# Converting each half of w1 and w2 in one set of instructions, with a later request for one v, and the look at the weights' range taken out of ScalarE's gaps

## The chip, the core and the metric

The kernel runs on one core of a Trainium2 chip. The core has a TensorE (PE, matrix products; its weight loads are listed as PEld), a VectorE (DVE), a ScalarE (ACT), a GpSimd (POOL) and a SyncE (SP), which here issues every DMA. The engines run side by side, each through its own list of instructions in order, and wait for each other by semaphores. The metric is the device time of one execution in microseconds; of the kernel before there are three runs, 464.53, 464.53 and 465.14 us, with a median of 464.53 us.

## What is computed

The reference has two parts. The first is a gated linear attention over 4 batches of 8 heads, 768 steps, head size 48:

```
f = 1 / (1 + exp(-f_logit))
for t in range(S):
    state = f[:, :, t, :, None] * state + einsum('bhd,bhe->bhde', k[:, :, t], v[:, :, t])
    y[:, :, t] = einsum('bhd,bhde->bhe', q[:, :, t], state)
```

Its result is laid out as x with 3072 rows and 384 columns, and goes through a feed-forward part whose only product of activations is elementwise:

```
a = x @ w1            # 384 x 1024
b = x @ w2            # 384 x 1024
h = a * b @ w3        # 1024 x 1024
out = h @ w_out       # 1024 x 384
```

The weights arrive as 64-bit floats. The kernel reads them as pairs of 32-bit words and makes 32-bit floats of them itself.

## The kernel before

**The work.** The sequence is cut into 24 chunks u = 0 to 23 of 128 steps. For each chunk DVE runs two scans over the gates (lines 523 and 545) and scales q and k by them (539, 553), PE multiplies the pairs within the chunk (566 or 576), ACT copies the products out (697 or 700), POOL masks them (706), PE multiplies them with v (604 or 650, 610, 669) and brings the state forward (622 or 683), DVE keeps the state (756, 759, 815), and ACT takes the result out (842). Four chunks make a block of 512 rows of x; there are six blocks. Block 0 is multiplied with w1 and w2 in plain products (`part`, line 894 with 256 columns), each pair of products being merged by one ACT copy (931) and one DVE product (936). Blocks 1 and 2 go through a scheme with seven products instead of eight (`seven`, line 990), blocks 3 to 5 through one with more sums and fewer products (`many`, line 1145), in which ACT copies partial results out of PSUM (1166) into a pool of temporaries named "t" and DVE adds them (1189). w3 and w_out are first multiplied with each other (`folding`, line 1477), and the last stage of each block uses that product (`down`, line 894 with 192 columns).

**The order.** Nothing is left to a scheduler at run time. Each piece of work is a task of class `Plan` with an engine, an estimated cost, its predecessors and a priority; `Plan.order` lists the tasks in the order in which they could start soonest, and the instructions are emitted in that order, for each engine its own list. Up to a planned time of `FULL` = 130 us the program puts in products of constants (`idle`, line 396) where the plan leaves PE without work.

**Converting the weights.** `fetch` (line 1367) loads one piece of a weight into a raw buffer and converts it. For w1 and w2, `weights` (line 1447) names four halves by letters: A is the first 512 columns of w1, B those of w2, C the last 512 columns of w1, D those of w2. Each half consists of three pieces of 128 rows and 512 columns, so twelve pieces in all, A0 to D2. A piece takes one DMA of 512 KB (line 1396), one ACT instruction on the low words (`rest`, 1415), and three DVE instructions of 512 columns: `shifted` (1418), `signed` (1422, which also needs ACT's result) and `joined` (1428). `EARLY = "23ACBD"` sets an order that the program enforces by dependencies: after DVE has prepared chunks 2 and 3 come A, C, B and D. w_out follows in four pieces of 768 columns and w3 in eight of 1024, through the same function. The tile `w12` holds w1 and w2 by matrix, group of 128 rows and column.

**The first loads.** SP issues the DMAs in the planned order: f, k, q and v of chunks 0 to 3 (lines 485, 489 and 472), with v of the fourth chunk (u = 3) behind its own q and ahead of A0. The load of v of chunk 3 writes into the tile `place`, and line 683 reads it from there.

**The looks.** The fast path holds only for weights within a range. `ranges` (line 1532) loads all weights again in 34 looks of 512 KB each (line 1544), and ACT goes twice over the high words of each, once for a sum of magnitudes (`total`, 1548) and once for a count (`count`, 1552). DVE turns the sums into one verdict (1560 to 1596), which is written to DRAM and read back (1586, 1590); PE's last product waits for it. In the kernel before, the looks rotate through three buffers, and their ACT tasks have `gap` set: `Plan.order` first lists everything with these tasks taken off ACT, collects ACT's idle gaps from that list, and puts each look's two instructions into gaps that are wide enough, from a planned time of 262 us on.

**The temporaries.** The pool "t" of `many` has nine places: two small tiles `firsts`, two strips `ups` within `place`, and five homes of tiles that are free by then.

Of the kernel before, what the change touches and what calls it, by code (L numbers as in the profile page):

```python
# [45 lines left out]
P = 128  # L46
C = 128
# [35 lines left out]
EARLY = "23ACBD"  # L83
CROWDED = [(6.0, 19.5, (1.35, 1.85)), (33.0, 46.0, (1.3, 1.3))]
# [4 lines left out]
GAP = 0.2  # L89
FILL_FROM = 262.0  # L90
RELOAD = 6.0
SPREAD = 10.0
# [34 lines left out]
class Plan:  # L127
# [16 lines left out]
    def add(self, eng, cost, emit, deps=(), prio=0.0, takes=(), frees=(), lag=0.2, slack=0.0, since=0.0, shared=False, gap=None):  # L144


        t = {
            "eng": eng, "cost": cost, "emit": emit, "deps": [d for d in deps if d is not None], "prio": prio,
            "takes": list(takes), "frees": list(frees), "lag": lag, "slack": slack, "since": since, "shared": shared, "at": None, "end": None, "no": len(self.tasks), "gap": gap,
        }  # L150
        self.tasks.append(t)
        return t

    def order(self):

        fill = [t for t in self.tasks if t["gap"] is not None]
        if fill:
            was = [(t["eng"], t["cost"]) for t in fill]
            for t in fill:
                t["eng"], t["cost"] = "none", 0.0  # L160
            slots, pools = ({n: (c, list(x)) for n, (c, x) in self.slots.items()}, {n: list(x) for n, x in self.pools.items()})
            busy = sorted((t["at"], t["end"]) for t in self.listed() if t["eng"] == "ACT" and t["cost"])
            for t in self.tasks:
                t["at"] = t["end"] = None
                t.pop("got", None)
            self.slots = {n: [c, x] for n, (c, x) in slots.items()}
            self.pools = pools
            for t, (t["eng"], t["cost"]) in zip(fill, was):
                pass
            gaps = [[a[1], b[0]] for a, b in zip(busy, busy[1:] + [(1e9, 1e9)]) if b[0] - a[1] > GAP]  # L170
            at = {}
            for t in fill:
                low = max([FILL_FROM] + [at[g] + w for g, w in t["gap"] if g in at])
                for g in gaps:
                    a = max(g[0], low)
                    if g[1] - a >= t["cost"] + GAP:
                        break
                t["since"], at[t["no"]], g[0] = a, a + t["cost"], a + t["cost"]
        return self.listed()

    def listed(self):
# [67 lines left out]
def kernel(  # L249
# [16 lines left out]
    w12 = const.tile([P, 2, KM, DFF], F32, name="w12")  # L266
# [10 lines left out]
def up_weights(w12, which, kc, jc):  # L277

    return w12[:, which, kc, jc * P : jc * P + P]
# [12 lines left out]
def ranged(ctx, tc, q, k, f_logit, v, w1, w2, w3, w_out, out, ident, w12, wc, left):  # L292
# [47 lines left out]
    halves = [a + i for a in (0, 2048, 4096, 8192, 10240) for i in (0, 1024)]  # L340
# [26 lines left out]
    plan.pool("t", len(homes) - NWT + 4)  # L367
# [16 lines left out]
    def temporary(i):  # L384

        if i < 2:
            return firsts[i]
        if i < 4:
            return ups[("u2", "u3")[i - 2]]
        return home(NWT + i - 4)  # L390
# [83 lines left out]
    def front(u):  # L474
# [4 lines left out]
        ask = [ask, ask + 0.5, ask + 1.0, n0 - (28.2, 28.2, 28.2, 28.2, 12)[min(u, 4)] if u in (0, 1) or u > 3 else ask + 1.2]  # L479
# [419 lines left out]
    def ffn(n):  # L899
# [190 lines left out]
        def w_view(i):  # L1090

            if i < KM * 4:
                return w12[:, :, i // 4].rearrange("p w (h g b c) -> p w h g b c", h=2, g=2, b=2)[:, :, i % 4 // 2, :, i % 2]
            return home(W_SUMS[i - 4 * KM][3]).rearrange("p (w g c) -> p w g c", w=2, g=2)
# [272 lines left out]
    def fetch(loads_, a, prio, subs, deps=()):  # L1367

        total = subs[-1][1]
        if not wide:
            def plain():
                for place_, src in loads_:
                    for c0, c1, dst, _, _ in subs:
                        d = dst().rearrange("p (a m) -> p a m", a=a)
                        m = (c1 - c0) // a
                        b0 = c0 // a if len(subs) > 1 else 0  # L1380
                        nc.sync.dma_start(d[place_], src[:, :, b0 : b0 + m])
            waits = [d for sub in subs for d in sub[4]]
            ld = plan.add("SP", 1.9 * total / 512, plain, waits, prio, lag=2.0)
            return [ld] * len(subs)
        load_no = len(users)
        if load_no < 2 * 2 * KM:
            where = halves[load_no % len(halves)]
        else:
            where = 2048 * ((load_no + 1) % NRAW)
        raw = at(where, 2 * total).bitcast(U32)  # L1390
        words = raw.rearrange("p (n two) -> p n two", two=2)
        held = holders(where, 2 * total)

        def load():
            for place_, src in loads_:
                nc.sync.dma_start(raw.rearrange("p (a m) -> p a m", a=a)[place_], src.bitcast(U32))

        ld = moves(1, total, 400, load, held + list(deps), prio, SURE, lanes=("lane", "heavy"))
        asked.append(ld)
        got = []  # L1400
        users.append((where, 2 * total, got))
        ends = []

        def sub(c0, c1, dst, due, waits):
            n = c1 - c0
            w = n / 512
            lo, hi = words[:, c0:c1, 0], words[:, c0:c1, 1]
            a0 = spot[0] if n <= 512 else (spot[0] + 512) // 1024 * 1024 % 2048
            spot[0] = (a0 + (512 if n <= 512 else 1024)) % 2048
            m = magnitudes[:, a0 : a0 + n]  # L1410
            mine = range(a0 // 512, (a0 + n + 511) // 512)
            s = {}

            def rest():
                nc.scalar.activation(lo.bitcast(F32), lo, AF.Copy, bias=2.0, scale=2.0**-51)  # L1415

            def shifted():
                nc.vector.tensor_scalar(m.bitcast(U32), hi, 3, None, ALU.logical_shift_left)

            def signed():  # L1420
                s["to"] = dst()
                nc.vector.scalar_tensor_tensor(
                    s["to"].bitcast(U32), hi, 0x80000000, lo, ALU.bitwise_and, ALU.bitwise_or
                )

            def joined():
                to = s["to"].bitcast(I32)
                nc.vector.tensor_tensor(to, m.bitcast(I32), to, ALU.add)

            past = [joins[i] for i in mine if i in joins]  # L1430
            e = plan.add("ACT", 0.2 + 0.43 * w, rest, [ld], due)
            h = plan.add("DVE", 0.16 + 0.27 * w, shifted, [ld] + past, due, shared=True)
            g = plan.add("DVE", 0.16 + 0.53 * w, signed, [e, h] + list(waits), due)
            j = plan.add("DVE", 0.16 + 0.53 * w, joined, [h, g], due - 1, shared=True)
            parts.append((g, j))
            joins.update({i: j for i in mine})
            got.append(g)
            ends.append(j)

        for one_ in subs:  # L1440
            sub(*one_)
# [580 lines left out]
```

## Time and profile before

| what | value |
| --- | --- |
| median of three runs | 464.53 us |
| the profiled execution: its own time | 464.53 us |
| the profiled execution: span from first to last instruction | 462.8 us |
| PE busy | 454.1 us, 98% of the span |
| DVE busy | 364.8 us, 79% |
| ACT busy | 208.2 us, 45% |
| POOL busy | 64.7 us, 14% |
| DMA moved | 68.75 MB |
| granted TensorE clock, mean | 0.998 |

The profile follows one execution. A line of the table of groups names the source line, the engine, the operation, what it writes and reads, how often, and the busy time and mean duration. A line of the timeline has the start in us from the span's start, the duration, the same names, and in brackets how long the engine had been idle before it and what ended that. PE's ends are modelled, so that a product's duration is not the distance to the next one; the distance of two starts is the better measure on PE. A DMA has an issue time on SP and a landing time, when its semaphore is counted up. A window gives busy time by engine in a stretch.

### The profile page before, as it was taken

The numbers are of one execution on the slowest core, as the hardware profiler recorded it, in microseconds if no ns is written. First come the engines' busy times: TensorE is split into PE (matmuls) and PEld (weight loads), VectorE is DVE, ScalarE is ACT, GpSimd is POOL, SyncE is SP. The second block draws the span as 40 slices with busy tenths as digits, with TensorE's granted clock in tenths as the row PEclk, the third lists the DMA queues.
The fourth block names the chain that finished last, engine by engine and source line by source line (L and its number), as shares of the span: only waits on it lengthen the run. The fifth ranks groups of instructions, "written<-read, shape, count | busy, mean of one in ns | idle before, by whom it ended". The sixth has DMA issues, their size and how long they took to land.

```text
span 462.8 us, 11767 instructions
## 1 busy us (share of the span) xinstructions
PE 454.1 (98%) x4800; PEld 395.6 (85%) x4800; DVE 364.8 (79%) x657; ACT 208.2 (45%) x468; POOL 64.7 (14%) x90
## 2 busy tenths in 40 slices
PE   8999999999999999999999999999999999999995
PEld 6778885666899888889998889998889988889995
DVE  8998999999898999989983598894669377767641
ACT  4565344532234444442432356664654666675000
POOL 9330001121122332322322000000000000000000
PEclk9999999999999999999999999999999999999999
DMA  6899899743246764445424335634135623330111
GB/s 181 269 297 306 268 343 276 260 103 87 80 110 192 205 186 113 133 135 166 120 57 113 111 112 178 221 113 149 47 124 176 200 91 92 90 95 0 35 68 40
DMA packets 43165, 68.75 MB, mean 149 GB/s; under 512 B 5201, under 2 KB 28242, under 8 KB 42082
## 3 DMA queue, kind: packets, MB, share of 16 engines
q1 hardware_dynamic: 43106, 67.95, 48.0%
q8 instruction: 39, 0.64, 0.6%
q14 instruction: 20, 0.16, 0.1%
HBM read 58.88 MB, written 9.04 MB: 147 GB/s over the span
## 4 chain that ended last, share of the span: by engine, by line
PE 93%; POOL 2%; DVE 2%; issue 1%; ACT 0%; POOLq 0%; DVEq 0%
PE f L894 26%; PE f L990 14%; PE f L1145 10%; PE f L1477 9%; PE pa L1145 7%; PE py L1145 5%; PE py L894 3%; PE py L650 3%; PE pa L894 3%; PE pa L576 2%; PE pa L683 2%; PE f L590 2%; PE py L669 2%; PE pa L990 1%; POOL ab L434 1%; PE f L396 1%
## 5 line engine op out<-in xcount | busy, mean ns | idle before, releaser
L706 POOL TENSOR_SCALAR_AFFINE_SELECT A<-A 64x512 f32<-64x512 f32 (+1 forms) x46 | 43.4, 943 | 104.0 <-ACT A L700 101.9
L1477 PE MATMUL f<-place 128*128 128x384 f32 x128 | 42.7, 488 | 0.0
L894 PE MATMUL f<-xt,w 128*128 128x256 f32 x192 | 42.1, 380 | 0.0
L894 PEld LDWEIGHTS f<-xt,w 128*128 128x128 f32 x192 | 36.3, 190 | 5.0
L894 PE MATMUL f<-place 128*128 128x192 f32 x216 | 39.5, 328 | 0.0
L1477 PEld LDWEIGHTS f<-place 128*128 128x128 f32 x128 | 23.8, 190 | 15.3
L894 PEld LDWEIGHTS f<-place 128*128 128x128 f32 x216 | 35.4, 190 | 0.5 <-issue 0.2
L990 PE MATMUL f<-xt,w 128*128 128x256 f32 x132 | 34.2, 379 | 0.0
L545 DVE TENSOR_TENSOR_SCAN bwd<-gate,back 112x512 f32<-112x512 f32 x24 | 30.8, 1285 | 0.7
L523 DVE TENSOR_TENSOR_SCAN fwd<-gate,floor 112x512 f32<-112x512 f32 x24 | 30.5, 1271 | 1.1 <-ACT gate L515 0.3
L990 PEld LDWEIGHTS f<-xt,w 128*128 128x128 f32 x132 | 24.8, 190 | 3.1
L842 ACT ACTIVATE ys<-py 112x512 f32<-112x512 f32 x22 | 13.1, 596 | 28.2 <-PE py L669 28.2
L1415 ACT ACTIVATE place<-place 128x512 f32<-128x512 uint32 (+2 forms) x24 | 21.1, 890 | 10.1 <-DMA place<-in_w_dram 7.9
L894 PE MATMUL f<-wc,ab 128*128 128x192 f32 x128 | 23.4, 326 | 0.0
L990 PE MATMUL f<-place 128*128 128x256 f32 x84 | 22.4, 385 | 0.0
L806 POOL TENSOR_TENSOR G<-lasts,gate 112x4 f32<-112x4 f32 x20 | 10.7, 535 | 81.3 <-ACT lasts L528 50.3
L894 PEld LDWEIGHTS f<-wc,ab 128*128 128x128 f32 x128 | 21.4, 190 | 0.4
L515 ACT ACTIVATE gate<-f 112x512 f32<-112x512 f32 x22 | 13.9, 632 | 15.4 <-DVE bwd L545 6.6
L650 PEld LDWEIGHTS py<-A,vt 64*64 64x64 f32 (+1 forms) x672 | 13.3, 127 | 7.3 <-issue 5.6
L650 PE MATMUL py<-A,vt 64*64 64x64 f32 (+1 forms) x672 | 18.1, 223 | 0.2
L1552 ACT ACTIVATE A<-A,back 128x512 f32<-128x512 f32 x23 | 17.9, 778 | 0.3
L990 PEld LDWEIGHTS f<-place 128*128 128x128 f32 x84 | 15.3, 190 | 2.2 <-ACT place L1031 0.2
(345 smaller groups left out, 1046.4 us busy)
## 6 DMA issues: line engine op xcount, KB each, us to landing
place<-in_w_dram SPq DMA_DIRECT2D x21, 512.0 KB, 6.4
A<-in_w_dram SPq DMA_DIRECT2D x19, 512.0 KB, 4.0
place<-in_w_dram SPq DMA_DIRECT2D x8, 1024.0 KB, 6.9
out_dram<-o SPq DMA_DIRECT2D x24, 192.0 KB, 2.3
q<-in_q_dram SPq DMA_DIRECT2D x46, 96.0 KB, 3.0
vt<-in_v_dram SPq DMA_DIRECT2D x23, 192.0 KB, 3.2
k<-in_k_dram SPq DMA_DIRECT2D x44, 96.0 KB, 2.5
yt<-ys SPq DMA_DIRECT2D x44, 96.0 KB, 2.9
```

Source lines behind the costliest of these rows:

```text
L515: nc.scalar.activation(gate[u % 2][:, 0:NQ], fu, AF.Sigmoid)
L523: nc.vector.tensor_tensor_scan(s["P"], gate[u % 2][:, 0:NQ], floor, 0.0, ALU.mult, ALU.max)
L545: nc.vector.tensor_tensor_scan(s["R"][:, ::-1], gate[u % 2][:, NQ:0:-1], back[:, ::-1], 0.0, ALU.mult, ALU.max)
L650: done = nc.tensor.matmul(y_block(u, hp, par, half)[p0 : p0 + w], lhsT=s["v"][half * W : half * W + W, h * D : h * D + w], rhs=s["A"][half ...
L706: nc.gpsimd.affine_select(out=a, in_=a, pattern=pattern, compare_op=ALU.is_ge, fill=0.0, base=0, channel_multiplier=-1,)
L842: nc.scalar.activation(ys, py, AF.Copy, accum_out=ysum[:, u : u + 1])
L894: nc.tensor.matmul(out_, lhsT=lhs[i], rhs=rhs[i], start=start and i == 0, stop=i == len(lhs) - 1, skip_group_check=True,)
L990: nc.tensor.matmul(q[nm][:, which * TH : which * TH + TH], lhsT=lhs[i](which), rhs=rhs[i], start=start and which == 0 and i == 0, stop=i = ...
L1145: nc.tensor.matmul(banks[g, c][:, which * TH : which * TH + TH], lhsT=lhs, rhs=x_node(a), start=first and which == 0, stop=True, skip_grou ...
L1415: nc.scalar.activation(lo.bitcast(F32), lo, AF.Copy, bias=2.0, scale=2.0**-51)
L1477: nc.tensor.matmul(w3s["p", jc], lhsT=w3s[jc][:, kc * P : kc * P + P], rhs=wos[:, kc], start=(kc == 0), stop=(kc == KF - 1),)
L1552: return lambda: nc.scalar.activation(a, a, AF.Sign, bias=small, accum_out=counts[:, i : i + 1])
```

## The change

Edits 1 and 2 concern the first conversion of the weights and the loads around it, edits 3 and 4 the second half of the kernel.

1. `fetch` takes a list of loads and converts all of them by one set of `shifted`, `signed`, `joined`. For w1 and w2 the list holds the three pieces of a half, so that DVE's three instructions run over 1536 columns and wait for all three loads. The DMAs and ACT's `rest` stay one per piece. `w12` is laid out by half, so that a half is contiguous. The halves lie in fixed places: A at 0, C at 3072, B at 8192, D at 0 again. For w_out and w3 each call has one load, as before.
2. v of the fourth chunk is asked for 2.05 planned units behind f instead of 1.2, which is behind A's loads. In SP's list it moves from ahead of the three loads of A to right behind all three.
3. The looks' ACT tasks are ordinary tasks, with a priority behind all others (500 + i instead of -400 + i); the second listing in `Plan.order` is gone. They have two buffers instead of three, the two halves of `both`, and the first two loads no longer wait for block 1's last products.
4. The pool "t" has seven places: two strips of `place` at 12864 (where the third look buffer was) and the five homes. The planned lateness of the two DMAs of the verdict is 20 instead of 10.

The core of the diff:

```
+VLATE = (1.2, 2.05)
+KQLATE = (0.5, 1.0)
+EARLY_AT = {"A": 0, "C": 3072, "B": 8192, "D": 0}
-GAP = 0.2
-FILL_FROM = 262.0
-RELOAD = 6.0
-SPREAD = 10.0
...
     def order(self):
-        fill = [t for t in self.tasks if t["gap"] is not None]
...
-        return self.listed()
-    def listed(self):
         free, done, left = dict.fromkeys(("PE", "DVE", "ACT", "POOL", "SP"), BEGIN), [], list(self.tasks)
...
-    w12 = const.tile([P, 2, KM, DFF], F32, name="w12")
+    w12 = const.tile([P, 2, 2, KM, KH * P], F32, name="w12")
...
-    plan.pool("t", len(homes) - NWT + 4)
+    plan.pool("t", len(homes) - NWT + 2)
...
-        if i < 2:
-            return firsts[i]
-        if i < 4:
-            return ups[("u2", "u3")[i - 2]]
-        return home(NWT + i - 4)
+        return at(12864 + TB * i, TB) if i < 2 else home(NWT + i - 2)
...
+    def fetch(loads_, where, prio, due, dst, waits=(), deps=()):
+        total = sum(n for _, n, _ in loads_)
...
+        for i, (at_, n, src) in enumerate(loads_):
+            def load(at_=at_, n=n, src=src):
+                nc.sync.dma_start(raw[:, 2 * at_ : 2 * (at_ + n)].rearrange("p (a m) -> p a m", a=src.shape[1]), src.bitcast(U32))
+            def rest(at_=at_, n=n):
+                part_ = lo[:, at_ : at_ + n]
+                nc.scalar.activation(part_.bitcast(F32), part_, AF.Copy, bias=2.0, scale=2.0**-51)
+            landed.append(moves(1, n, 400, load, held + list(deps), prio + 0.02 * i, SURE, lanes=("lane", "heavy")))
+            low.append(plan.add("ACT", 0.2 + 0.43 * n / 512, rest, [landed[-1]], due + 0.02 * i))
...
+        h = plan.add("DVE", 0.16 + 0.27 * w, shifted, landed + past, due, shared=True)
+        g = plan.add("DVE", 0.16 + 0.53 * w, signed, [*low, h] + list(waits), due)
+        j = plan.add("DVE", 0.16 + 0.53 * w, joined, [h, g], due - 1, shared=True)
...
         for item in (x for x in EARLY if x in "ABCD"):
...
-                for kc in range(KM):
-                    c0 = half * KH * P
-                    src = w[kc * P : kc * P + P, c0 : c0 + KH * P].unsqueeze(1)
-                    pieces[which, half] += fetch(
...
+            pieces[which, half] = fetch(
+                [(kc * KH * P, KH * P, w[kc * P : kc * P + P, cols].unsqueeze(1)) for kc in range(KM)],
+                EARLY_AT[item], turn_of(item), due[which, half],
+                lambda which=which, half=half: w12[:, which, half].rearrange("p k c -> p (k c)"),
+            )
...
-            ld = moves(1, LOOK, 400, load(i), last[:1] + [q["m3"] for q in blk[1]["seven"]] if i < 3 else last[i - 2 : i - 1], 500 + i, SURE_W, since=LOOKS)
-            a = plan.add("ACT", 0.92, total(i), [ld], -400 + i, gap=[(last[-1]["no"], 0.0)] + ([(last[i - 2]["no"], RELOAD)] if i > 2 else []))
-            last.append(plan.add("ACT", 0.95, count(i), [a], -400 + i, gap=[(a["no"], 0.0)]))
+            ld = moves(1, LOOK, 400, load(i), last[:1] if i < 2 else last[i - 1 : i], 500 + i, SURE_W, since=LOOKS)
+            a = plan.add("ACT", 0.92, total(i), [ld], 500 + i)
+            last.append(plan.add("ACT", 0.95, count(i), [a], 500 + i))
...
-            sent = moves(1, 0.4, 250, told, [looked], 0, SPREAD)
+            sent = moves(1, 0.4, 250, told, [looked], 0, 20.0)
```

## The prediction

> **What bounds the kernel now.** I read the busy shares, the 40 slices and the chain that ended last, then windows, to see whether PE's share is even.
>
> ```profile
> PE 454.1 (98%) x4800; PEld 395.6 (85%) x4800; DVE 364.8 (79%) x657; ACT 208.2 (45%) x468; POOL 64.7 (14%) x90
> ...
> PE 93%; POOL 2%; DVE 2%; issue 1%; ACT 0%; POOLq 0%; DVEq 0%
> ```
>
> ```profile
> 20.00:40.00 20.00, 18.86 (x342) 16.26 (x343) 18.76 (x37) 11.85 (x26) 3.78 (x4) 1.00 0.96 325
> 40.00:60.00 20.00, 20.00 (x95) 17.60 (x94) 17.28 (x31) 8.75 (x16) 0.20 (x1) 1.00 0.85 275
> ...
> 260.00:280.00 20.00, 20.00 (x95) 17.60 (x94) 17.70 (x31) 9.95 (x24) 0.00 (x0) 1.00 0.28 95
> 400.00:420.00 20.00, 20.00 (x96) 17.64 (x96) 13.22 (x25) 13.36 (x29) 0.00 (x0) 1.00 0.28 80
> ```
>
> The columns are length, PE, PEld, DVE, ACT and POOL busy, granted clock, DMA share, GB/s. PE is full from 40 us on, and it really is full: the starts of PE's products lie as far apart as their shape allows (0.433 us for a product of 256 columns, 75 of them from 35.26 to 67.74), and after 258 us all stalls together come to about 1.2 us (the largest 0.46 us at 337). So a saving on DVE or ACT is worth nothing in itself. Only three things can change the time: when the full stretch begins, stalls that come or go in it, and the tail. The order of PE after the change holds the same products and the same 24 `idle` products, so PE's work is equal. The place to look at is PE's timeline before 40 us:
>
> ```profile
> 26.39 1.00 PE L650 MATMUL py<-A,vt 64*64 64x64 f32 x32
> ...
> 28.13 0.27 PE L683 MATMUL pa<-place,kt 64*48 64x48 f32 x5
> 29.27 0.60 PE L683 MATMUL pa<-place,kt 64*64 64x48 f32 x27 [0.86 <-issue]
> 29.80 1.56 PE L396 MATMUL f<-floor 112*128 112x256 f32 x6
> 31.20 1.03 PE L894 MATMUL f<-xt,w 128*128 128x256 f32 x4
> ```
>
> From 31.20 PE has weights products. Just before come three `idle` products (six records), and a hole of 1.08 us from 28.19 to 29.27 that the profile puts down to nothing ("issue"). The trace's packets explain it: a 16,384-byte packet of queue q8 ("instruction" on the page), started at 26.86 and done at 27.92; PE went on 1.35 us later. I read the hole as PE waiting for its own code, behind data loads (DMA share 0.96 here).
>
> **Edit 1: sets of 1536 columns.** DVE's rows, start to start:
>
> ```profile
> 33.26 0.41 DVE L1418 TENSOR_SCALAR place<-place 128x512 uint32<-128x512 uint32 x1
> 33.59 0.68 DVE L1422 SCALAR_TENSOR_TENSOR w<-place 128x512 uint32<-128x512 uint32 x1
> 34.31 0.69 DVE L1428 CUSTOM_DVE_ANT_0 w<-place,w 128x1024 uint16<-128x1024 uint16 x1
> 34.92 0.42 DVE L1418 TENSOR_SCALAR place<-place 128x512 uint32<-128x512 uint32 x1
> ...
> 65.65 1.23 DVE L1428 CUSTOM_DVE_ANT_0 place<-place 128x2048 uint16<-128x2048 uint16 x1
> 66.79 0.42 DVE L936 TENSOR_TENSOR ab<-f,ab 128x256 f32<-128x256 f32 x1
> 67.12 0.69 DVE L1418 TENSOR_SCALAR place<-place 128x1024 uint32<-128x1024 uint32 x1
> 67.72 1.22 DVE L1422 SCALAR_TENSOR_TENSOR place<-place 128x1024 uint32<-128x1024 uint32 x1
> 68.98 1.23 DVE L1428 CUSTOM_DVE_ANT_0 place<-place 128x2048 uint16<-128x2048 uint16 x1
> ```
>
> Three instructions take 1.66 us for 512 columns (33.26 to 34.92) and 0.60 + 1.26 + 1.14 = 3.00 us for 1024, so 1.34 us per further 512 and an estimated 4.34 us for 1536 (0.87 + 1.80 + 1.67). Three pieces took 4.98. A half saves 0.64, the four halves 2.6 us of DVE. ACT and the DMAs do the same work.
>
> Does PE see it? A half is ready only when its last load is in. By the trace's landing records A0 to A2 came in at 21.05, 23.13 and 24.42, C2 at 29.37, B2 by 37.3 (its ACT instruction starts there).
>
> *A:* with v of chunk 3 out of the way A2 lands about 0.5 us sooner, 23.9. DVE is free at 23.56. Set: 23.9 + 0.87 = 24.8; then the three state instructions, which stood at 24.49 to 25.94 before (1.45), end at 26.2; + 1.80 + 1.67 = 29.7. Before, A was done at 29.95.
> *B:* its three instructions start at B2's landing, 37.2 + 0.9 + 1.8 + 1.7 = 41.5. Before, 41.6. PE needs B after eight products of three matmuls and one `values`: 30.8 + 24 x 0.433 + 1.4 = 42.5. Cover 1.0 us.
> *D and w_out:* w_out's first raw buffer now overlaps D's, so its load waits for D's `signed`: 41.5 + 0.9 + 1.8 = 44.2, about 45 with D's last landing, instead of its issue at 41.88. What hides the 3 us is block 0's products, which keep PE busy until 68; without that cover it would cost those 3 us.
>
> So edit 1 gives PE nothing at A (PE isn't waiting there) and nothing at B. Bounds: a gain of 0 (PE was not late for the weights), a loss from B2 landing later than its cover, below.
>
> **The `idle` products.** In the new order PE gets four instead of three at 25.0, and two instead of three at 29.8. One product (0.43 us) moves from behind the hole to ahead of it. If the hole ends when the code arrives, at 29.27 as before, the extra product fills part of it, and the weights' products start 0.43 us earlier, at 30.77; A (29.7) allows that. If the hole came 0.43 us later with the same length, the gain is 0; if there is none, it is 1.08. I take 0.43, because the packet's time, not PE's, sets the end in the row.
>
> The Trainium skill (page "Runtime: NRT & Kernel Launch", section "Instruction fetch mechanics") says that an engine's code is fetched in 16 KiB blocks over a DMA queue of its own, the next block while the current one executes, and that the fetch is hidden. The packets' size agrees; the 1.08 us hole speaks against "hidden". By the page's word the hole would be something else and might simply move, and the sum would be 0 instead of -0.43 us.
>
> **Edit 2: v of chunk 3 later.** It was issued at 13.81 and landed at 18.11; behind A's 1.5 MB it lands at about 24.4, in the place where A2 was. Its first reader is line 683 at 28.1. Cover 3.7 us; cost 0. Behind it on SP stand v of chunk 4 (read after 70 us) and C, in equal order. The gain is the 0.5 us of A2, which A doesn't pass on.
>
> **Edit 3: looks without gaps.** In ACT's new list the 34 looks (0.683 + 0.192 and 0.778 + 0.192, so 0.88 and 0.97 us) stand among 79 copies instead of 94; 43 copies stand right behind a look in both lists. Of the 72 copies of line 1166 (12 in each of six groups of 34 products, 29.3 us) thirteen come after the last look, so the looks end some 35 us before their 428 of now; the verdict (DVE 429.16 to 430.89, 1.7 us) moves into `many` with it, and its two DMAs (8.8 us, 431.00 to 439.84) go out while no store waits behind them on SP. What matters is whether a look makes a copy late for PE. In `many` three chains take turns at 0.863 us a product, so a bank is wanted again 1.73 us after its product ended. A copy begins 0.2 us after that end (336.72 to 336.92), takes 0.59, and PE goes on 0.05 us later: 0.84 is used, 0.89 left. A look ahead costs at most 0.97 - 0.89 = 0.08 us of PE. So: best 1.2 us gained (present stalls gone), worst 43 x 0.08 = 3.4 us lost, plus late reloads with two buffers (before: two waits, 1.8 us). I take 0, the end that the 0.08 us is nearest to; PE's new order still has a run of 61 products of `many` (52 us) with nothing put between.
>
> **Edit 4: seven temporaries.** A copy that finds no place waits for a DVE sum (0.69). PE's new order doesn't draw `down` products ahead to fill holes, so I take 0; the bound is one such wait per group, 6 x 0.69 = 4.1 us.
>
> **Sum.** -0.43 (hole) + 0 + 0 + 0. The profiled execution took 464.53 us, 1.73 more than its span, and equals the median: 464.1 us. The tail (from 458.1, the last product, to 462.8) has the same instructions.
>
> **Rivals.** *R1, the hole closes* (-1.08) and late stalls shrink (up to -1.2): 462.3 to 463.5, say 463.3. For it: DMA order around 27 us changes. Against: as many bytes are queued there. *R2, looks ahead of copies*: half the bound plus one late reload, 1.7 + 0.9, so 466.7. It decides once a copy waits longer than 0.89 us: two looks in a row ahead of one copy (18 places in the new list, 12 in the old), or a look whose load is late, with ACT's copies queued behind it and PE behind them. Against: loads land in 4.0 us (median). *R3, the last landing rules*: B2 in, or its ACT instruction, over 1.0 us later than I reckon, with all of B behind it; PE stands before its first w2 product. 3 us late gives 464.1 + 2.0 = 466.1. *R4, seven places are too few*: half of 4.1, 466.2. *R5, nothing arrives*: the hole moves along, 464.5; this lies in my forecast's band.
>
> **Chances.** A run of this kernel can tell 0.2% (0.93 us) from no change, so "same" is 463.6 to 465.46. Forecast with R5 0.42, R1 0.20, R2 0.22, R3 0.10, R4 0.06. Faster 0.20, same 0.42, slower 0.38. The forecast's own band is 463.6 to 465.4. For 8 in 10 I go down to 462.9 (R1's late stalls only half gone) and up to 467.6 (R2's bound nearly whole).
>
> **What would show it.** Right: three DVE instructions of 1536 columns near 0.9, 1.8, 1.8 us; a hole in line 683 ending near 29.3, shorter than 1.08; first L894 near 30.8; PE at 20.00 in every window from 40 to 440; looks over by about 395. Wrong: PE waiting for DMA or DVE line 1381 (new numbering) before 45 us; ACT's copies behind a look with PE idle after 258; a window of PE below 19.5.

## The result and the profile after

The changed kernel takes 465.72 us (median of 22 executions), the kernel before 464.72 us beside it: a ratio of 1.0021, with a 95% interval of 1.0011 to 1.0030. The forecast was 464.1 us and "same" the likeliest; it came out slower, by about 1.0 us. The profiled execution after has a span of 463.5 us (before: 462.8).

First the page, then windows of the kernel after (length, then busy us and instructions of PE, PEld, DVE, ACT and POOL, granted clock, DMA share, GB/s):

```profile
PE 454.9 (98%) x4800; PEld 396.5 (86%) x4800; DVE 362.9 (78%) x633; ACT 208.2 (45%) x468; POOL 67.4 (15%) x90
...
PE 94%; POOL 2%; DVE 1%; issue 1%; ACT 1%; POOLq 0%; DVEq 0%
```

```profile
20.00:40.00 20.00, 19.61 (x345) 16.93 (x346) 18.04 (x21) 12.14 (x26) 4.46 (x4) 1.00 0.91 312
40.00:60.00 20.00, 20.00 (x95) 17.60 (x94) 16.70 (x25) 7.77 (x16) 1.03 (x1) 1.00 0.85 287
...
360.00:380.00 20.00, 19.06 (x96) 17.01 (x95) 8.64 (x17) 12.04 (x29) 0.00 (x0) 1.00 0.43 138
380.00:400.00 20.00, 19.70 (x92) 17.02 (x91) 14.76 (x26) 13.82 (x31) 0.00 (x0) 1.00 0.44 131
```

The two late windows of the kernel before:

```profile
360.00:380.00 20.00, 20.00 (x100) 18.01 (x99) 9.62 (x19) 12.15 (x27) 0.00 (x0) 1.00 0.43 143
380.00:400.00 20.00, 20.00 (x94) 17.44 (x93) 16.15 (x29) 13.41 (x29) 0.00 (x0) 1.00 0.29 88
```

Two things moved, in opposite directions. From 20 to 40 us PE gained 0.75 us of busy time (18.86 before). From 360 to 400 us it lost 1.24 us: before, both windows were at 20.00.

To add such losses up I take every distance between two starts on PE and subtract what its shape usually takes (0.216 us for one pass over 256 columns). What remains after 258 us, called **late stalls** below, is 1.56 us before and 2.92 us after: 1.36 us more. Early, the first weights product starts at 30.51 in place of 31.20, 0.69 us sooner. Together +0.67 us, which is the difference of the spans.

The early part on PE (start, duration, then the operation; line 617 was 650, 650 was 683, 363 was 396, 861 was 894):

```profile
28.12 0.64 PE L543 MATMUL pa<-Q,K 48*64 48x64 f32 x32
28.58 1.03 PE L650 MATMUL pa<-place,kt 64*48 64x48 f32 x32
29.55 1.13 PE L363 MATMUL f<-floor 112*128 112x256 f32 x4
30.51 1.24 PE L861 MATMUL f<-xt,w 128*128 128x256 f32 x5
```

The hole in the product of the state has shrunk from 1.08 us to 0.31 (28.64 to 28.95), too short for the timeline to break the group. DVE's sets of half A, then half B:

```profile
25.89 1.75 DVE L1375 SCALAR_TENSOR_TENSOR w<-place 128x1536 uint32<-128x1536 uint32 x1
27.68 1.76 DVE L1381 CUSTOM_DVE_ANT_0 w<-place,w 128x3072 uint16<-128x3072 uint16 x1
```

```profile
36.00 0.96 DVE L1371 TENSOR_SCALAR place<-place 128x1536 uint32<-128x1536 uint32 x1 [1.12 <-DMA place<-in_w_dram]
37.32 1.76 DVE L1375 SCALAR_TENSOR_TENSOR w<-place 128x1536 uint32<-128x1536 uint32 x1 [0.35 <-ACT place L1356]
39.11 1.76 DVE L1381 CUSTOM_DVE_ANT_0 w<-place,w 128x3072 uint16<-128x3072 uint16 x1
```

A is joined at 29.44 and B at 40.87. DVE now stands 1.12 us for B2's landing, and no product of PE is late for it.

The late part, PE and then ACT around the largest stall (line 1112 was 1145, the copies' line 1133 was 1166, 1492 is a look):

```profile
370.59 1.89 PE L1112 MATMUL py<-xt,w 128*128 128x256 f32 x8
372.32 1.03 PE L1112 MATMUL pa<-place,k 128*128 128x256 f32 x4
374.29 1.13 PE L1112 MATMUL py<-xt,q 128*128 128x256 f32 x4 [0.94 <-ACT ys L1133]
```

```profile
372.52 0.59 ACT L1133 COPY Q<-py 128x512 f32<-128x512 f32 x1 [1.14 <-PE py L1112]
373.00 0.67 ACT L1492 ACTIVATE A<-A 128x512 f32<-128x512 f32 x1
373.57 0.20 ACT L1492 ACTIVATION_READ_ACCUMULATOR A<-A 128x1 f32 x1
373.66 0.58 ACT L1133 COPY ys<-py 128x512 f32<-128x512 f32 x1
```

PE's product at 374.29 waits for the copy that ends at 374.24; a look stands ahead of that copy. That much is what the second rival described. The smaller stalls of 0.46 us at 337 and 391 have no look directly ahead of the copy, and they needed another explanation.

### The profile page after: what moved, and what is told of

Same layout as the page of the kernel before. It is cut to its first block, busy times and chain, and to the rows that moved or that the text cites. A ratio compares the mean times of both kernels' runs of the same rounds, so it can differ in the third digit from the quotient of the medians.

```text
span 463.5 us, 11766 instructions
## 1 busy us (share of the span) xinstructions
PE 454.9 (98%) x4800; PEld 396.5 (86%) x4800; DVE 362.9 (78%) x633; ACT 208.2 (45%) x468; POOL 67.4 (15%) x90
## 4 chain that ended last, share of the span: by engine, by line
PE 94%; POOL 2%; DVE 1%; issue 1%; ACT 1%; POOLq 0%; DVEq 0%
PE f L861 24%; PE f L957 15%; PE f L1112 12%; PE f L1420 9%; PE py L1112 6%; PE pa L861 5%; PE pa L1112 5%; PE py L861 4%; PE py L617 3%; PE pa L543 2%; PE pa L650 2%; PE f L557 2%; PE py L636 2%; PE py L957 1%; POOL ab L401 1%; PE f L363 1%
## 5 line engine op out<-in xcount | busy, mean ns | idle before, releaser
L861 PE MATMUL f<-xt,w 128*128 128x256 f32 x192 | 42.1, 380 | 0.0
L861 PEld LDWEIGHTS f<-xt,w 128*128 128x128 f32 x192 | 36.3, 190 | 5.0
L1420 PEld LDWEIGHTS f<-place 128*128 128x128 f32 x128 | 23.9, 190 | 15.5
L957 PE MATMUL f<-xt,w 128*128 128x256 f32 x140 | 36.2, 380 | 0.0
L861 PE MATMUL f<-place 128*128 128x192 f32 x176 | 32.0, 327 | 0.0
L957 PEld LDWEIGHTS f<-xt,w 128*128 128x128 f32 x140 | 26.3, 190 | 3.5
L861 PEld LDWEIGHTS f<-place 128*128 128x128 f32 x176 | 28.9, 190 | 0.3 <-issue 0.2
L1496 ACT ACTIVATE A<-A,back 128x512 f32<-128x512 f32 x34 | 26.5, 781 | 0.5
L1492 ACT ACTIVATE A<-A 128x512 f32<-128x512 f32 x34 | 23.3, 686 | 5.7 <-DMA A<-in_w_dram 5.7
L773 POOL TENSOR_TENSOR G<-lasts,gate 112x4 f32<-112x4 f32 x20 | 12.5, 627 | 74.1 <-ACT lasts L495 28.8
L861 PE MATMUL f<-wc,ab 128*128 128x192 f32 x112 | 20.7, 328 | 0.0
L861 PEld LDWEIGHTS f<-wc,ab 128*128 128x128 f32 x112 | 18.6, 190 | 0.3
```

Of the source, the lines that this page charges most:

```text
L861: nc.tensor.matmul(out_, lhsT=lhs[i], rhs=rhs[i], start=start and i == 0, stop=i == len(lhs) - 1, skip_group_check=True,)
L957: nc.tensor.matmul(q[nm][:, which * TH : which * TH + TH], lhsT=lhs[i](which), rhs=rhs[i], start=start and which == 0 and i == 0, stop=i = ...
L1420: nc.tensor.matmul(w3s["p", jc], lhsT=w3s[jc][:, kc * P : kc * P + P], rhs=wos[:, kc], start=(kc == 0), stop=(kc == KF - 1),)
L1492: return lambda: nc.scalar.activation(a, a, AF.Abs, accum_out=sums_[:, i : i + 1])
L1496: return lambda: nc.scalar.activation(a, a, AF.Sign, bias=small, accum_out=counts[:, i : i + 1])
```

## Experiments

Each kernel ran beside the kernel before; ratios are to it. "First" is the start of the first weights product, "late" the late stalls, both of the profiled execution.

| kernel | ratio, 95% interval | first, us | late, us |
| --- | --- | --- | --- |
| before | 1 | 31.20 | 1.56 |
| after | 1.0021 [1.0011, 1.0030] | 30.51 | 2.92 |
| sets_and_v | 0.9988 [0.9978, 0.9998] | (34.12) | (2.77) |
| sets_and_v_again | 0.9988 [0.9969, 1.0006] | 31.06 | 1.45 |
| looks_only | 1.0035 [1.0022, 1.0048] | (33.03) | 3.01 |
| after_nine | 1.0022 [1.0003, 1.0042] | 30.61 | 2.94 |
| gaps_two_nine | 1.0077 [1.0055, 1.0099] | 30.60 | 1.32 |
| v_only | 0.9997 [0.9982, 1.0012] | 30.81 | 1.18 |
| sets_only | 1.0010 [0.9998, 1.0021] | not used | 2.34 |
| idle_moved | 1.0000 [0.9989, 1.0011] | 30.87 | 1.56 |
| before_idle_out | 0.9994 [0.9982, 1.0007] | 29.96 | 1.56 |
| last_idle_out | 0.9964 [0.9953, 0.9975] | 30.13 | 1.44 |
| empty_looks | 1.0010 [0.9998, 1.0022] | 30.92 | 2.28 |
| ungapped_three | 1.0048 [1.0032, 1.0064] | 31.35 | 4.41 |
| no_looks | 1.0023 [1.0007, 1.0039] | 30.98 | 3.04 |
| unplanned_looks | 1.0167 [1.0144, 1.0189] | 30.22 | 9.95 |
| no_looks_nine | 1.0020 [1.0000, 1.0039] | 30.39 | 2.68 |
| no_looks_six | 0.9955 [0.9938, 0.9972] | 30.26 | 0.30 |
| sets_and_v_six | 0.9964 [0.9950, 0.9978] | 30.83 | 0.31 |
| last_idle_out_six | 0.9948 [0.9927, 0.9969] | 29.66 | 0.29 |

The profiled executions of sets_and_v and looks_only had a slowed clock for 6.8 and 3.4 us near 33 us, so their bracketed figures are not compared.

### The change in two halves

sets_and_v is the changed kernel with the late part of before (gaps, three look buffers, nine temporaries); looks_only is the kernel before with the late part of the change.

```diff
 # sets_and_v, against the changed kernel
-            a = plan.add("ACT", 0.92, total(i), [ld], 500 + i)
+            a = plan.add("ACT", 0.92, total(i), [ld], -400 + i, gap=[(last[-1]["no"], 0.0)] + ([(last[i - 2]["no"], RELOAD)] if i > 2 else []))
...
-    plan.pool("t", len(homes) - NWT + 2)
+    plan.pool("t", len(homes) - NWT + 4)
```

> The changed kernel with only its early part: sets of 1536 columns and the later v of chunk 3; the looks stand in ACT's planned gaps again, with three buffers and nine temporaries as before. Every engine's order up to 258 us is that of the changed kernel. Theory (two effects that add: the start of PE's full stretch 0.69 us earlier, by the two traces, and 1.36 us more of PE stalls after 258 us, which come from the looks): span 462.8 - 0.7 = 462.1, time 0.15% less than before, first product of line 861's kind near 30.5, PE's stalls after 258 us together near 1.6 us. Rival (the early gain is lost again before the end in any case, by work that is paced by other engines): span 462.8, no change.

> The kernel before with only the late part of the change: looks ordinary in ACT's list, two buffers for them, seven temporaries; all before 258 us is in the order of the kernel before. Theory (the late loss stands by itself): span 462.8 + 1.4 = 464.2, time 0.3% more than before, with PE stalls after 258 us near 2.9 us, each ahead of a product whose bank an ACT copy frees behind a look. Rival (the loss comes only with the new order of the early part, by its phase): span 462.8, no change.

Both came out as the theory had them, and they add: 0.9988 x 1.0035 = 1.0023, against 1.0021 for the whole change. The early part gains 0.12% (sets_and_v_again reads the same, but its interval takes in no change at all), the late part loses 0.35%.

### Which part of the late loss is it?

after_nine and gaps_two_nine give back, one after the other, the nine temporaries and the gaps; ungapped_three keeps nine temporaries and three buffers and lets the looks stand anywhere.

```diff
 # ungapped_three, against sets_and_v
-            a = plan.add("ACT", 0.92, total(i), [ld], -400 + i, gap=[(last[-1]["no"], 0.0)] + ([(last[i - 2]["no"], RELOAD)] if i > 2 else []))
+            a = plan.add("ACT", 0.92, total(i), [ld], 500 + i)
```

> The changed kernel with nine temporaries instead of seven; PE's, SP's and GpSimd's orders are the same as in the changed kernel, some of ACT's copies and DVE's sums change places. Theory (the looks ahead of copies make the loss): the stalls after 258 us stay, span 463.0 to 463.9. Rival (seven places are too few: a copy waits for a place): the stalls of 1.1 us at 373 and 0.5 us at 391 go, span 462.1. Rival (late reloads with two buffers): as the theory, 463.5, and ACT still waits 5 us or more on the loads of the looks.

> The changed kernel with looks put into ACT's planned gaps as before and nine temporaries, but still two look buffers instead of three. Theory (a look put into a gap smaller than itself makes a copy late): stalls after 258 us near 1.6 us as before, span 462.1, 0.15% less than before. Rival (late reloads with two buffers): ACT waits on look loads as in the changed kernel, stalls stay near 2.9 us, span 463.5.

> The early part of the change, nine temporaries and three look buffers as before, but the looks as ordinary tasks in ACT's list, in whatever gap comes, instead of planned gaps that hold them. Theory A (position: a look in a gap smaller than itself makes a copy late): stalls after 258 us near 2.5 us or more, time 0.2% above before, as the changed kernel. Theory B (two buffers: a look whose load is late holds the copies queued behind it): with three buffers ACT's waits for look loads fall below 2 us, stalls near 1.6 us, time 0.15% below before.

The temporaries make no difference under the change's order: 1.0022, with the same stalls. Two buffers do not make the loss either: with three, ACT waits 1.4 us in all for the looks' loads (5.7 us in the changed kernel), the looks are over at 361 us (406), and PE loses more, 4.41 us. The two buffers slow the looks down, which may well help, but since ungapped_three has another order too, that is not shown. gaps_two_nine has short late stalls as the theory had them, 1.32 us, and yet is the slower by 0.77%: gaps and two buffers together let the looks go on to 443.8 us, and the kernel's end waits for their verdict; the profiled execution shows 2.1 us of it (a span of 464.9 against 462.8). DVE in gaps_two_nine:

```profile
455.87 0.36 DVE L1300 TENSOR_TENSOR o<-f,place 128x192 f32<-128x192 f32 x1 [0.94 <-PE f L896]
458.16 0.27 DVE L1574 TENSOR_REDUCE least<-row 1x1 f32<-1x128 f32 x1 [1.93 <-DMA row<-good]
458.47 0.14 DVE L1575 TENSOR_SCALAR left<-least 1x1 int32<-1x1 f32 x1
459.34 0.36 DVE L1308 TENSOR_TENSOR o<-f,place 128x192 f32<-128x192 f32 x1 [0.73 <-DVE left L1575]
```

PE is done at 457.13, earlier than before's 458.08, but the last result stands behind the verdict, and the span is 464.9. Looks that end 30 us ahead of PE's last product (before: 428.5) cost nothing at the end; looks that end 13 us ahead of it do. So the earlier end in the changed kernel is worth nothing.

### The looks' own price

empty_looks keeps every order of the changed kernel and takes ACT's 68 instructions of the looks out; no_looks takes them out of the planner's reckoning too; unplanned_looks does them, but gives them no time in the planner's list.

```diff
 # empty_looks, against the changed kernel (total; count alike)
-            return lambda: nc.scalar.activation(a, a, AF.Abs, accum_out=sums_[:, i : i + 1])
+            return lambda: None
 # no_looks, on top of it
-            a = plan.add("ACT", 0.92, total(i), [ld], 500 + i)
+            a = plan.add("ACT", 0.0, total(i), [ld], 500 + i)
```

> The changed kernel without ScalarE's 68 instructions of the looks: the check of the weights' range is left out (its sums and counts are set to passing values by two memsets); the loads of the looks are still issued, and every other instruction stands in the same order on its engine. The loads no longer wait for a look, so they come earlier. Theory (looks stand ahead of copies that PE waits for): the stalls at 337, 373 and 391 us all go, span 463.5 - 1.9 = 461.6, time 0.2% below before. Rival (the order of copies and sums itself, or the seven temporaries, make the stalls): stalls of 1.1 and 0.5 us stay, 0.2% above before.

> The changed kernel with looks that take no time in the planner's list and are not done: the check of the weights' range is left out (two memsets give passing values); two look buffers for the loads and seven temporaries stay. Theory (the stalls that stayed without the looks' work come from a list in which looks take ACT's time): stalls after 258 us fall from 1.9 to 1.3 us or less, span near 462, time 0.1 to 0.15% less than before. Rival (seven temporaries or the loads make them): stalls stay near 1.9 us, 0.1% above before, as empty_looks.

> The changed kernel with looks that are done, but take no time in the planner's list; PE's order is that of no_looks. Theory (a look ahead of a copy delays PE by what the copy's cover lacks, and the planner cannot keep looks off such places here): stalls well above those of no_looks, 2.5 us or more after 258 us, time 0.2% or more above before. Rival (only the order that the planner makes of the looks' time costs, the looks themselves nothing): as no_looks, 0.1% less than before.

My theory (it is all the looks) fell at empty_looks. PE and ACT of empty_looks at the place shown above:

```profile
373.94 1.13 PE L1112 MATMUL py<-xt,q 128*128 128x256 f32 x4 [0.30 <-ACT ys L1133]
```

```profile
372.82 0.59 ACT L1133 COPY Q<-py 128x512 f32<-128x512 f32 x1 [1.14 <-PE py L1112]
373.30 0.59 ACT L1133 COPY ys<-py 128x512 f32<-128x512 f32 x1
```

The look's 0.64 us are gone (2.92 to 2.28 late), and 0.46 us stay, here and at the two other places. The second theory (a list made for the looks) fell at no_looks: 3.04 us late with no look in the list or on ACT. unplanned_looks confirms that looks cost where nobody places them: 6.9 us more than no_looks.

### What makes PE late against its own plan

The planner's list holds PE idle for 0.11 us after 240 us in no_looks as in sets_and_v, so the stalls are something that it doesn't reckon with. The rows of the changed kernel at 337 us show what, PE and then ACT:

```profile
334.31 1.11 PE L1112 MATMUL py<-xt,w 128*128 128x256 f32 x4
335.25 1.03 PE L1112 MATMUL py<-place,k 128*128 128x256 f32 x4
336.11 1.03 PE L1112 MATMUL f<-xt,w 128*128 128x256 f32 x4
337.44 1.13 PE L1112 MATMUL py<-xt,q 128*128 128x256 f32 x4 [0.30 <-ACT place L1133]
```

```profile
336.31 0.59 ACT L1133 COPY ys<-py 128x512 f32<-128x512 f32 x1 [1.42 <-PE py L1112]
336.80 0.59 ACT L1133 COPY place<-py 128x512 f32<-128x512 f32 x1
```

`pa` and `py` are tiles of two PSUM banks each. By the list, the copy at 336.31 reads the product of 334.31, done at about 335.4, and the next copy that of 335.25, in the tile's other bank. The first copy starts 0.03 us after the *second* product's end (335.25 + 1.03), ACT having been idle for 1.42 us; in ACT's list the second copy has no wait for PE of its own, since the first one's covers it. And PE's product at 337.44, which needs the first copy's bank, waits for the second copy. Both banks are waited for as one. (In the kernel, `py` is one tile of shape 128 x 2 x 512, and each of its two halves serves as a bank.)

The last four kernels test this. In the kernels named "six" the late part uses one bank of each of these tiles, six banks in all; the planner's list is as long as with eight.

```diff
-            plan.pools["f"] += [late] * 4
+            plan.pools["f"] += [late] * 2
...
-            nm = ("pa", "py")[(plan.got - NF) // 2]
+            nm = ("pa", "py")[plan.got - NF]
...
-            return found[nm][:, plan.got % 2]
+            return found[nm][:, 0]
```

> no_looks (the check of the weights' range left out) with six PSUM banks in the late part in place of eight: of the tiles pa and py, which hold two banks each, one is used. The planner's list is as long as with eight. Theory (a wait on one bank of such a tile is a wait on both): stalls after 258 us fall from 2.9 us to 1.0 or less, time 1.5 to 2 us below no_looks. Rival (seven temporaries, or too few banks now): stalls stay near 2.9 or grow.

> no_looks with nine temporaries in place of seven, eight banks; PE's order is the same. Theory (banks that share a tile): stalls stay at 2.9 us, time as no_looks. Rival (seven places): stalls fall to 1.5 us or less.

> sets_and_v (early part of the change, looks in gaps, three look buffers, nine temporaries) with six PSUM banks in the late part. Theory (banks that share a tile): the stalls of 0.73 us at 355 and 0.13 us at 422 go, together 1.3 us falls to 0.5 or less, time 0.8 us below sets_and_v, 0.3% below before. Rival (too few banks): new stalls, 0.1% below before or worse.

No theory of this study was answered more plainly: 0.30, 0.31 and 0.29 us late in the three kernels, with no single stall left over 0.09 us, and 0.68% less time than no_looks (0.9955 against 1.0023). Nine places in no_looks take 0.36 us off its late stalls and leave the rest (1.0020). One window of sets_and_v_again, with eight banks, then sets_and_v_six, both with all the looks on ACT:

```profile
340.00:360.00 20.00, 19.42 (x111) 18.33 (x110) 14.66 (x31) 11.87 (x29) 0.00 (x0) 1.00 0.64 191
```

```profile
340.00:360.00 20.00, 20.00 (x117) 19.33 (x116) 15.56 (x34) 12.81 (x33) 0.00 (x0) 1.00 0.61 201
360.00:380.00 20.00, 20.00 (x100) 18.06 (x99) 10.37 (x20) 12.39 (x29) 0.00 (x0) 1.00 0.41 135
380.00:400.00 20.00, 20.00 (x95) 17.60 (x94) 15.73 (x30) 13.70 (x31) 0.00 (x0) 1.00 0.30 89
```

And no_looks, then no_looks_six:

```profile
380.00:400.00 20.00, 19.03 (x87) 16.12 (x86) 14.32 (x26) 8.05 (x15) 0.00 (x0) 1.00 0.00 1
```

```profile
380.00:400.00 20.00, 20.00 (x94) 17.62 (x93) 15.69 (x29) 7.93 (x14) 0.00 (x0) 1.00 0.00 1
```

Another order of work is not what removes the stalls. In the traces of no_looks and no_looks_six, and again of sets_and_v_again and sets_and_v_six, PE, ACT and DVE go through the same instructions in the same order from 258 us on; only the banks differ. Fewer banks alone would leave a product fewer places to go to, so the gain belongs to the tiles that are no longer shared. A kernel with eight banks in eight tiles of their own was not built. The Trainium skill (page "PSUM — Partial Sum Buffer", section "PSUM bank collisions raise a hardware error") asks for a guard by bank and quadrant, or simply by bank. What stood here was wider than that, two banks, and the difference is what the rows price.

### The early gain

v_only and sets_only each do one part of the early change; idle_moved moves the one `idle` product alone; the two "idle_out" kernels drop those that stand directly ahead of the first weights product.

```diff
 # v_only, against the kernel before
-        ask = [ask, ask + 0.5, ask + 1.0, n0 - (28.2, 28.2, 28.2, 28.2, 12)[min(u, 4)] if u in (0, 1) or u > 3 else ask + 1.2]
+        ask = [ask, ask + 0.5, ask + 1.0, n0 - (28.2, 28.2, 28.2, 28.2, 12)[min(u, 4)] if u in (0, 1) or u > 3 else ask + (2.05 if u == 3 else 1.2)]
 # idle_moved, against the kernel before (the planner's counts were 5, 2, 3, 3)
-                idle(n)
+                idle(counts.pop(0))
```

The counts are 5, 2, 4, 2 in idle_moved, 5, 2, 3, 0 in before_idle_out and, from sets_and_v's 5, 2, 4, 2, 5, 2, 4, 0 in last_idle_out; two more products near 124 us stay in all of them.

> The kernel before with the later v of chunk 3 and nothing else. PE's order gets four and two idle products in place of three and three, as in the changed kernel; the weights are still converted in pieces of 512. Theory (the early gain is the idle product that moves ahead of the wait for code, which goes with the request for v, not with the sets): time 0.10 to 0.15% less than before; a hole in the product of line 683 that ends about 1.3 us behind the 16,384-byte packet of queue q8; first weights product of line 894 near 30.5 to 30.8. Rival (the sets make the early gain): no change.

> The kernel before with sets of 1536 columns and nothing else: v of chunk 3 ahead of A as before, looks in gaps, three look buffers, nine temporaries. PE's order keeps three and three idle products. Theory (the early gain goes with v): no change, ratio 1.000 within 0.001, first weights product near 31.2. Rival (the sets make the early gain, by DVE's 2.6 us): 0.15% less than before.

> The kernel before with one idle product of PE moved from behind the wait for code to ahead of it (four and two in place of three and three); nothing else changes on any engine. Theory (the wait ends about 1.3 us behind the code's packet, whatever PE did before): first weights product of line 894 0.43 us earlier after a packet at the same time, hole shorter by 0.43, time 0.09% less than before. Rival (the hole moves along with PE): hole of the same length, first weights product at the same distance from the packet as before, no change.

> The kernel before without the last three idle products ahead of the first weights product. Theory (these three, 1.3 us, are PE's own time between the wait for code and the weights; A is joined at 29.95, line 683 done at 29.84): full stretch begins near 30.05 instead of 31.20, time 0.25% less than before. Rival (PE then waits further on, for w2's half B that DVE joins at 41.6 to 43.2 or for the folding's inputs at 67 us): part or all of it comes back as stalls at 41 to 43 or 67 us, no change.

> The early part of the change (sets and the later v, the looks as before) without the last two idle products ahead of the first weights product. Theory: full stretch begins near 29.7 instead of 30.5, time 0.85 us less than that kernel's, 0.3% less than before; B is joined at 40.9 and needed at 41.7. Rival (the start is passed on to a stall at B, or at the folding near 67.5 us): as that kernel, 0.12 to 0.15% less than before.

> The kernel of sets_and_v unchanged, so that the two kernels without idle products have it beside them on the same chip, and for a second reading of the early gain. Theory: 0.15% less than before, hole of 0.3 to 1 us, first weights product 0.4 to 0.7 us earlier than before. Rival (the early gain was that day's packet): 0 to 0.05% less.

sets_only is not the kernel that it was meant to be: PE's products of lines 652 and 685 came out interleaved, and it computes something else than the reference; nothing is concluded from it. That the four and two `idle` products go with v is read from v_only's order. Which of the two makes the gain of 0.12% the times don't tell: v_only has 0.9997 and both together 0.9988, with intervals that overlap, and v_only's own takes in no change. PE in idle_moved:

```profile
28.69 0.27 PE L683 MATMUL pa<-place,kt 64*48 64x48 f32 x3
29.30 0.66 PE L683 MATMUL pa<-place,kt 64*48 64x48 f32 x29 [0.34 <-issue]
29.90 1.13 PE L396 MATMUL f<-floor 112*128 112x256 f32 x4
30.87 0.60 PE L894 MATMUL f<-xt,w 128*128 128x256 f32 x2
```

The code's packet ends at 27.91 here and at 27.92 before; the hole ends at 29.30 and 29.27; PE came to it 0.56 us later, and the hole is 0.52 us shorter. The first weights product starts 0.33 us sooner. In 17 of the 19 profiles read for it the hole ends 1.30 to 1.55 us behind the packet's end, which itself lies anywhere from 27.49 to 29.86; in the two others (unplanned_looks and no_looks_six, packets done at 27.26 and 26.7) PE comes too late to see a hole. So the step is shown in the trace, but its size is below what the times resolve (1.0000 for idle_moved), and each execution draws another packet: with four and two, the first weights product lay between 30.22 and 31.35 (sets_and_v, with its late packet, apart).

Dropping the `idle` products gives what the theory says where A is early enough. In last_idle_out the first weights product starts 0.93 us sooner than in sets_and_v_again, and the time falls by 1.1 us (463.22 against 464.36, on one chip). In before_idle_out it starts 1.24 us sooner than before, but within the folding (82.41 against 83.30) only 0.89 is left, and the time shows 0.06%, within its interval.

### A version that beats both

> last_idle_out with six PSUM banks in the late part. Theory: the gains add, 0.36% + 0.17% = 0.5% less than before, span near 460.6. Rival: as last_idle_out, 0.35% less.

The gains add as far as can be told: 0.9948 [0.9927, 0.9969], 462.09 us against 464.42; the rival's 0.35% lies inside the interval too, but the late stalls of 0.29 us in place of 1.44 speak for the sum. Its PE from the hole on:

```profile
28.67 1.02 PE L685 MATMUL pa<-place,kt 64*48 64x48 f32 x32
29.66 3.69 PE L896 MATMUL f<-xt,w 128*128 128x256 f32 x16
```

## Why the prediction was wrong, point by point

**What bounds the kernel: right.** PE's full stretch, its start and its stalls carry the whole difference of the two traces. DVE's busy time fell by 1.9 us and nothing came of it.

**Edit 1, the sets, worth 0: right as far as the runs tell.** A set took 0.96 + 1.75 + 1.76 = 4.47 us, against 4.34 estimated. A was joined at 29.44 (29.7 forecast), B at 40.87 (41.5), w_out's first load issued at 44.13 (45), all of it covered as the prediction said. (From their terms as printed, the forecast's 41.5 and 42.5 for B come to 41.6 and 42.6; the cover of 1.0 us stays.)

**The idle products and the hole, -0.43 us: right in mechanism, near in size (idle_moved's trace has 0.33), and too small for the times to show.** The hole's end follows the packet, as taken. The profiled execution shows -0.69 because its packet also ended 0.27 us earlier (27.65). The Trainium skill's sentence (page "Runtime: NRT & Kernel Launch", section "Instruction fetch mechanics") that fetching is hidden does not hold in these executions, and the sum of 0 that went with it was the worse one; idle_moved's time alone could not have told.

**Edit 2, v later, cost 0: right.** Line 650 never waits for it. What the prediction did not see is that the moved `idle` product belongs to this edit and not to the sets.

**Edit 3, looks without gaps, taken as 0: the step that failed.** The prediction reckoned that a bank is wanted again 1.73 us after its product ended, that a copy uses 0.84 of it and that 0.89 are left, so that a look ahead "costs at most 0.97 - 0.89 = 0.08 us of PE". It read this cover from the copy at 336.92, taking the product that ended at 336.72 for the copy's own. The rows of the kernel before, PE and then ACT, show that it wasn't:

```profile
334.92 1.11 PE L1145 MATMUL pa<-place,k 128*128 128x256 f32 x4
335.86 1.03 PE L1145 MATMUL pa<-xt,w 128*128 128x256 f32 x4
338.05 1.13 PE L1145 MATMUL pa<-xt,K 128*128 128x256 f32 x4 [0.30 <-ACT ys L1166]
```

```profile
336.92 0.59 ACT L1166 COPY place<-pa 128x512 f32<-128x512 f32 x1 [1.32 <-PE pa L1145]
337.41 0.59 ACT L1166 COPY ys<-pa 128x512 f32<-128x512 f32 x1
```

Two products of `pa` come one after the other, and then two copies out of it. By the kernel's list the first copy's own product is the one of 334.92, which ended at 335.86 by the prediction's measure (the next one's start); yet the copy starts only behind the second product. The bank is wanted 1.73 us after 335.86, at 337.59; PE goes on at 338.05, behind the second copy: 0.46 us late, without a look just ahead. So the row from which 0.89 us of cover was taken has none; it is the very stall of 0.46 us at 337 that the prediction names as the largest and leaves unexplained. Where a bank shares its tile with another one in turn, the copy starts only after the next product, about 0.9 us later; the cover is then gone without any look (stalls of 0.46 us), and a look in between costs nearly in full: 0.64 us at 373. Late stalls rose by 1.36 us. Of these 0.64 are a look ahead of a copy (empty_looks); the other 0.72 are two more waits of 0.46 us on paired banks (in the stall at 373, and at 391), less smaller stalls that only the old order had. That these waits come from the paired banks is seen in the changed kernel's rows at 337, and rests on three other kernels with six banks, which have none of them; the changed kernel itself was not run with six. That the old order met fewer such places by anything but luck was not shown: planned without looks, the order has 3.04 us of them.

The looks end at 406 us and not at 395, and the end of the kernel does not wait for them.

**Edit 4, seven temporaries, taken as 0: right** for this change (after_nine); 0.36 us in no_looks.

**The rivals.** R2 named the place, a copy late behind a look, and the price was 2.6 us against 1.36 measured; its condition, a copy that waits more than 0.89 us, was met, but what used the 0.89 up was not two looks or a late load. ACT does wait longer for loads (5.7 us against 1.8), and ungapped_three shows that this isn't the loss. R1's first half came true in the profiled execution (0.31 us of hole), its second half turned round. R3, R4 and R5 did not occur: B2 landed at 35.92, before the 37.2 forecast.

**The sum.** -0.43 and 0 were forecast; -0.69 and +1.36 are what the two traces show, and 1.0 us is what the times show. The sign that would give it away, "a window of PE below 19.5", stands at 360:380 with 19.06.

## What to carry to other kernels

A cover is read at the place where it is to be used, and from the product whose result is copied: a copy that starts 0.2 us after one product may have been held since an earlier one, whose bank lies in the same tile. When an engine stands although its planner plans no wait, compare the start of the waiting instruction with the ends of *all* writers of the same tile, and look whether the instruction behind it has a wait of its own. And filler ahead of a stage that has become ready earlier is worth removing: two constant products were worth 0.24% here, more than the change's early part itself.

## What the runs showed of the hardware

A hole of PE can cost more than its length. In sets_and_v and looks_only the code's packet came 2.0 and 1.1 us later than before, the holes were 2.51 and 2.06 us long, and the clock fell to half, 1.6 us into the hole in sets_and_v and 1.1 us after its end in looks_only: in looks_only PE's window of 32 to 34 us has a granted clock of 0.50, and one pass over 256 columns took 0.427 us in place of 0.216 for 3.4 us, in sets_and_v for 6.8 us. A hole of 1.22 us (before_idle_out) left the clock alone. The Trainium skill (page "TensorE: Matmul & The Clock Gate", section "HAM oscillation — how this bites in real kernels") puts the limit for idle stretches at about 3.4 us; here 2.06 us was enough, with short 64-row products on both sides of it.

What sets the time of the code's packet, whose end lay anywhere from 26.70 to 29.86 us in executions of the same early order, stayed open.
